# Attention's low product with 64 weight columns, and transposes set between matrix products

## The chip, the cores and the metric

The kernel runs on one core of a Trainium2 chip. The metric is the device time of one execution in microseconds (us), as the median of several runs. A profiled execution of the same program gives the span from its first to its last instruction and the times of every instruction; TensorE's instructions stand there as two rows of work, the matrix products (PE) and their weight loads (PEld).

## The reference

Attention whose mask comes from hash buckets, and behind it two feed-forward blocks with full matrices:

```python
q_bits = (np.einsum('bhsd,dk->bhsk', q, proj) > 0)      # 6 bits, likewise for k
mask = q_bucket[:, :, :, None] == k_bucket[:, :, None, :]
scores = scale * np.matmul(q, k.transpose(0, 1, 3, 2))   # 2 x 8 heads, 768 x 768, head size 64
scores = np.where(mask, scores, -1000000000.0)
attn = np.exp(scores - np.max(scores, axis=-1, keepdims=True))
attn = attn / (np.sum(attn, axis=-1, keepdims=True) + 1e-09)
x = np.matmul(attn, v)                                   # -> 1536 tokens x 512
h = np.maximum(x @ w_in, 0.0);  x = h * h @ w_out        # first block, width 2048
h = x @ w_in2;  y = (h / (1 + np.exp(-h))) @ w_out2      # second block
```

## The kernel before

TensorE multiplies operands that were rounded to a shorter format (fp32r). To keep precision the kernel splits a number into a high part and a low part (the rest) and adds the products of the parts.

The 16 heads are worked on as 8 pairs. A pair is 4 units (2 heads, 2 halves of 384 queries), so there are 32 units, and a unit holds three blocks of 128 queries. Attention is a loop over steps d, from -5 to 97, written out by hand; a step issues work of several units at different stages. One ordinary step holds:

- on TensorE: `transp` (L772) of two key blocks g and g+1, each three 128x128 transposes of the exponentials P into one PSUM tile t; then `av` (L793) of two key blocks that were transposed two steps earlier; then `score_mm` (L734), four products for one query block into a PSUM tile s. The mask's bits are extra rows of the second two of these products.
- on VectorE (DVE): `row_max` (L748) of the score tile of the step before, the low parts of two transposed blocks (`t_lo`, L788), and the two small operations of `row_live` (L752, L753).
- on ScalarE (ACT): the high parts of two transposed blocks (`t_hi`, L782), the exponential of one score tile (`score_exp`, L761), whose last instruction reads the accumulated row sums, and after the last key block of a unit a copy of its output (`ob`, L812).

`av` multiplies P's high part th (L801) and its low part tl (L802) by the same weights: v's high half beside v's low half, 64 + 64 = 128 columns. Rows 0 to 63 of the output tile o collect P times v's high half, rows 64 to 127 P times v's low half; two DMAs and a sum add them later.

Once in a pair, in its step `long[d]`, `bits_mm` (L527) computes the hash bits of the next pair: for each half z six products with 48 weight columns, z = 0 into a tile bs and z = 1 into a tile bt (`ops`, L530). VectorE turns them into mask values (`bits_cmp`, L540), and small DMAs put these into the operands of the next pair's scores (`place_bits`, L661). In six of these seven steps TensorE then runs `rb_mm` (L827): six 128x128 transposes that lay the reciprocal row sums of an older pair along the tokens, into a tile rb, which ScalarE copies out (`x_norm`, L842).

The tiles s, bs and rb share one pool of two PSUM buffers (`ps_s`, L466). They take turns: bs takes the buffer of the score tile before last, rb that of the last score tile, and can be written only after `score_exp` has read that tile. Each engine works through its own list in program order. TensorE's list is read ahead of its array, and a wait there holds what stands behind it.

After attention the feed-forward blocks run, in an order that a planner (`Plan`, L53) makes; the change does not touch them.

Of the kernel before, what the change touches and what calls it, by code (L numbers as in the profile page):

```python
# [444 lines left out]
def lsh_attention_moe_moe(ctx, tc, kd, qk, qf, fq, v, pc, wi1, wo1, wi2, wo2, out):  # L445
# [81 lines left out]
    def bits_mm(p):  # L527
# [4 lines left out]
        for z in range(2):  # L532
            for j, (w, x) in enumerate(ops):
                mm(s[z][0:48, 0:QW], w, x[:, z * QW : (z + 1) * QW], start=j == 0, stop=j == 5)  # L534
# [237 lines left out]
    def transp(g, t=None):  # L772
        u, kt = divmod(g, KT)
        if t is None:
            t = ps_t.tile([128, 512], F32, tag="t", name=f"t{g}")
        for j in range(3):
            nc.tensor.transpose(t[:, j * 128 : (j + 1) * 128], P[u, j][:, kt * 128 : (kt + 1) * 128], ident)  # L777
        PT[g] = (t,)
# [14 lines left out]
    def av(g):  # L793
        u, kt = divmod(g, KT)
        p, h, z = u // 4, (u // 2) % 2, u % 2
        if kt == 0:
            otile[u] = ps_o.tile([128, 512], F32, tag="o", name=f"o{u}")
        o = otile[u]
        vv = pair[p]["vv"][:, h * KT + kt].rearrange("p a d -> p (a d)")
        th, tl = PT.pop(g)  # L800
        mm(o[:, 0:QW], vv, th, start=kt == 0, stop=False)  # L801
        mm(o[:, 0:QW], vv, tl, start=False, stop=kt == KT - 1)  # L802
        if kt == KT - 1:
            if p not in xs:
                xs[p] = [a1.tile([128, S], F32, tag=n, bufs=b, name=f"{n}{p}") for n, b in (("ta", 2), ("tb", 1))]
            if u == NU - 1:
                ta, zs = xs[p][0], slice(z * QW, (z + 1) * QW)
                nc.scalar.copy(out=ta[64:128, zs], in_=o[0:64, 0:QW])
                nc.vector.tensor_tensor(out=ta[64:128, zs], in0=o[64:128, 0:QW], in1=ta[64:128, zs], op=ALU.add)
                return  # L810
            ob = a2.tile([128, QW], F32, tag="ob", name=f"ob{u}")
            nc.scalar.copy(out=ob, in_=o[:, 0:QW])  # L812
            for i in range(2):
                nc.sync.dma_start(out=xs[p][i][64 * h : 64 * h + 64, z * QW : (z + 1) * QW], in_=ob[64 * i : 64 * i + 64])
# [11 lines left out]

    def rb_mm(p):  # L827
        s = ps_s.tile([128, 2, 512], F32, tag="s", name=f"rb{p}")
# [3 lines left out]
        return s  # L832
# [97 lines left out]
    with tc.manual_schedule():  # L930
# [66 lines left out]
        for d in range(-5, G // 2 + 3):  # L997
# [10 lines left out]
            for fn, a in mid.pop(d, []):  # L1008
                fn(*a)
            if 0 <= g < G and d in (92, 94):  # L1010
# [114 lines left out]
```

## Time and profile before

| what | value |
|---|---|
| median of 3 runs | 740.75 us (740.70 to 743.93) |
| span of the profiled execution | 739.4 us |
| PE, PEld busy | 732.1 us (99%), 627.3 us (85%) |
| DVE, ACT, POOL busy | 610.0 us (83%), 461.6 us (62%), 249.6 us (34%) |
| `av`, high part L801 | 192 products, 72.5 us busy |
| `av`, low part L802 | 192 products, 64.5 us busy |
| transposes of P, L777 | 576, 79.1 us busy |
| transposes of `rb_mm`, L831 | 42, 5.7 us busy |
| products of `bits_mm`, L534 | 84 |
| attention's last TensorE work, feed-forward's first | about 235.6 us into the span |
| TensorE clock granted | full in all of 40 slices |

Busy times of products overlap, since each is shown from its start to the modelled end of a pipeline; the distance from one start to the next is what one costs. In a row of several like instructions ("x6") the time runs from the first start to the last end.

### The profile page before, as it was taken

What the parts mean: (1) busy time and instruction counts of PE and PEld (TensorE: products, weight loads), DVE (VectorE), ACT (ScalarE), POOL (GpSimd) and SP (SyncE); (2) the same over time, 40 slices, a digit from 0 to 9 for tenths busy, and PEclk for the clock granted to TensorE, in tenths of its full rate; (3) what the DMA queues carried; (4) which work ended last, traced back from release to release, by engine and by line L of the source; (5) the groups of instructions that cost most, each with busy time, mean ns of one, the idle gap of its engine ahead of it and who ended that gap; (6) DMA issues with size and microseconds to landing.
All of it is one profiled execution on the core that took longest, in us unless ns stands there. A gap on an engine that the chain in (4) does not pass through costs nothing.

```text
span 739.4 us, 10895 instructions
## 1 busy us (share of the span) xinstructions
PE 732.1 (99%) x3734; PEld 627.3 (85%) x3735; DVE 610.0 (83%) x1152; ACT 461.6 (62%) x866; POOL 249.6 (34%) x219
## 2 busy tenths in 40 slices
PE   8999999999999999999999999999999999999998
PEld 4799999999998888888888888888888888888887
DVE  6899999999999998887878896788888777776442
ACT  7888998998896882773566278366335525623510
POOL 7547477877674104103103103500330320230000
PEclk9999999999999999999999999999999999999999
DMA  6987787686462113311320220002133024010012
GB/s 180 210 175 151 182 186 176 154 186 148 115 157 60 57 60 111 114 59 57 114 86 24 91 86 28 29 28 87 58 99 129 30 78 150 1 58 1 1 71 100
DMA packets 27687, 71.87 MB, mean 97 GB/s; under 512 B 4208, under 2 KB 9120, under 8 KB 27632
## 3 DMA queue, kind: packets, MB, share of 16 engines
q1 hardware_dynamic: 24872, 64.52, 31.4%
q0 software_dynamic: 2160, 5.90, 3.9%
q10 hardware_dynamic: 600, 0.75, 0.4%
q8 instruction: 30, 0.49, 0.3%
q14 instruction: 25, 0.20, 0.1%
HBM read 49.80 MB, written 3.15 MB: 72 GB/s over the span
## 4 chain that ended last, share of the span: by engine, by line
PE 95%; DVE 2%; DMA 2%; ACT 1%; issue 0%; SPq 0%; DVEq 0%; ACTq 0%
PE bank L341 35%; PE bank L260 21%; PE bank L231 12%; PE s L741 8%; PE t L777 8%; PE o L802 4%; PE o L801 4%; PE bt L534 1%; DMA fr<-in_dram 1%; PE bs L534 1%; DMA kk<-bt 1%; PE rb L831 1%; DVE tl L788 1%; DVE mt L748 1%; ACT P L761 0%
## 5 line engine op out<-in xcount | busy, mean ns | idle before, releaser
L160 POOL TENSOR_TENSOR wp<-wt,wp 128x512 fp32r<-128x512 f32 x56 | 78.2, 1407 | 329.5 <-ACT wp L158 307.5
L260 PE MATMUL bank<-xb,wp 128*128 128x512 f32 x480 | 110.1, 389 | 0.0
L788 DVE TENSOR_TENSOR tl<-t,th 128x384 fp32r<-128x384 f32 x192 | 104.8, 548 | 2.4 <-ACT th L782 2.2
L260 PEld LDWEIGHTS bank<-xb,wp 128*128 128x128 f32 x480 | 90.1, 188 | 18.7
L761 ACT ACTIVATE P<-s,mt 128x768 f32<-128x768 f32 x96 | 95.6, 996 | 10.6 <-DVE mt L753 7.1
L748 DVE TENSOR_REDUCE mt<-s 128x1 f32<-128x768 f32 x96 | 91.4, 952 | 5.5 <-PE s L741 4.9
L741 PE MATMUL s<-kk,qq 76*128 76x384 f32 (+1 forms) x384 | 84.5, 341 | 1.6 <-DMA kk<-bt 0.8
L782 ACT CAST th<-t 128x384 fp32r<-128x384 f32 x192 | 82.2, 483 | 4.0 <-PE t L777 3.4
L158 ACT CAST wp<-wt 128x512 fp32r<-128x512 f32 x56 | 34.2, 619 | 78.2 <-DVE wt L215 44.5
L231 PE MATMUL bank<-x0h,wp 128*128 128x512 f32 x256 | 80.2, 389 | 0.0
L777 PE MATMUL t<-ident,P 128*128 128x128 f32 x576 | 79.1, 272 | 1.0 <-DVE tl L788 0.9
L777 PEld LDWEIGHTS t<-ident,P 128*128 128x128 f32 x576 | 67.8, 140 | 5.7 <-DVE tl L788 1.1
L801 PE MATMUL o<-th,vv 128*128 128x384 f32 x192 | 72.5, 377 | 0.0
L741 PEld LDWEIGHTS s<-kk,qq 76*128 76x128 f32 (+1 forms) x384 | 67.8, 188 | 4.3 <-ACT P L761 2.1
L265 DVE TENSOR_TENSOR ts<-bank,ts 128x512 f32<-128x512 f32 x80 | 54.4, 690 | 19.8 <-PE bank L260 17.2
L802 PE MATMUL o<-tl,vv 128*128 128x384 f32 x192 | 64.5, 336 | 0.2 <-DVE tl L788 0.2
L245 ACT ACTIVATE ts<-bank 128x512 f32<-128x512 f32 x48 | 28.6, 596 | 49.4 <-PE bank L260 28.9
L231 PEld LDWEIGHTS bank<-x0h,wp 128*128 128x128 f32 x256 | 48.1, 188 | 9.9
L160 DVE TENSOR_TENSOR gql<-ts,gqh 128x512 fp32r<-128x512 f32 x64 | 43.8, 703 | 8.9 <-ACT gqh L158 8.9
L173 ACT ACTIVATE wt<-raw 128x512 f32<-128x512 f32 x58 | 38.1, 671 | 20.2 <-POOL wp L160 17.6
L341 PE MATMUL bank<-wol,gqh 128*128 128x512 f32 (+1 forms) x132 | 50.5, 383 | 0.0
L341 PE MATMUL bank<-woh,gql 128*128 128x512 f32 (+1 forms) x132 | 50.5, 383 | 0.0
(185 smaller groups left out, 1631.7 us busy)
## 6 DMA issues: line engine op xcount, KB each, us to landing
raw<-in_dram SPq DMA_DIRECT2D x64, 512.0 KB
kk<-in_dram POOLq DMA_DIRECT2D x15, 384.0 KB, 6.1
qq<-hq SPq DMA_DIRECT2D x28, 192.0 KB
vr<-in_dram SPq DMA_DIRECT2D x8, 384.0 KB
ta<-ob SPq DMA_DIRECT2D x31, 96.0 KB
tb<-ob SPq DMA_DIRECT2D x31, 96.0 KB
out_dram<-ts SPq DMA_DIRECT2D x11, 256.0 KB
rq<-in_dram SPq DMA_DIRECT2D x7, 384.0 KB
```

The lines of the kernel that those rows point to most:

```text
L160: add(("DVE", "POOL")[pool], l, lambda: eng.tensor_tensor(out=lo(), in0=src(), in1=hi().bitcast(F32), op=ALU.subtract), (*rk, *hk), lk, po ...
L231: mm(bank[b], w[:, x, op, sl], t["x0"][y][:, kt], start=kt == 0 and j == 0, stop=kt == 3 and j == 2)
L260: mm(bank[b], w[:, p, op, k * 128 : k * 128 + 128], x[:, q, xop, k], start=first and k == 0 and j == 0, stop=k == 1 and j == 2, skip_group ...
L341: mm(bank[b][:, 0:wd], x, y, start=i == 0 and n == 0, stop=i == FB - 1 and n == 2)
L741: mm(s[:, n, 0:QW], t["qq"][h][0:kk, ab, c0 : c0 + 128], t["kk"][h][0:kk, ab, n * QW : (n + 1) * QW], start=ab == 0, stop=ab == 1)
L748: nc.vector.tensor_reduce(out=m[:, 0:1], in_=s[:, :, 0:QW], op=ALU.max, axis=AX.XY, negate=True)
L761: nc.scalar.activation(out=e.rearrange("p (a b) -> p a b", a=2), in_=s[:, :, 0:QW], func=AF.Exp, scale=m[:, 1:2], bias=m[:, 2:3], accum_ou ...
L777: nc.tensor.transpose(t[:, j * 128 : (j + 1) * 128], P[u, j][:, kt * 128 : (kt + 1) * 128], ident)
L782: nc.scalar.copy(out=th, in_=PT[g][0][:, 0:QW])
L788: nc.vector.tensor_tensor(out=tl, in0=t[:, 0:QW], in1=th.bitcast(F32), op=ALU.subtract)
L801: mm(o[:, 0:QW], vv, th, start=kt == 0, stop=False)
L802: mm(o[:, 0:QW], vv, tl, start=False, stop=kt == KT - 1)
```

## The change

The two products of `av` are taken apart. `av_hi` is the old product of P's high part with 128 weight columns. `av_lo` multiplies P's low part by v's high half alone, 64 weight columns into the upper 64 rows of o; the product of the two low parts is no longer computed. `av_out` is the rest of `av`.

In 92 steps the order on TensorE becomes another: the three transposes of block g and the first of block g+1 as before, then `av_hi` of the first block, a transpose, `av_lo` of the first, a transpose, `av_lo` of the second, and `av_hi` of the second behind all of them. In steps 92 and 94, and where no transposes are left, the order is high, low, low, high.

`rb_mm` becomes a generator. Where it shares a step with `bits_mm`, one of its six transposes is issued ahead of each of the six products of the half z = 1; where it does not, all six follow as before.

```diff
--- before.py
+++ after.py
@@ -524,13 +524,15 @@
         nc.sync.dma_start(out=t["qq"][h][0:64, 1, :].bitcast(F32), in_=t["lp"][rows, 0].bitcast(F32))
         nc.sync.dma_start(out=t["kk"][h][64:128, 0, :].bitcast(F32), in_=t["lp"][rows, 1].bitcast(F32))
 
-    def bits_mm(p):
+    def bits_mm(p, between):
         t = pair[p]
         hp, lp = t["hp"], t["lp"]
         ops = [(w[:, 48 * i : 48 * i + 48], x) for i in range(2) for (w, x) in ((pjh, hp[i]), (pjl, hp[i]), (pjh, lp[:, i]))]
         s = ps_s.tile([128, 2, 512], F32, tag="s", name=f"bs{p}")[:, 0], ps_t.tile([128, 512], F32, tag="t", name=f"bt{p}")
         for z in range(2):
             for j, (w, x) in enumerate(ops):
+                if z:
+                    next(between, None)
                 mm(s[z][0:48, 0:QW], w, x[:, z * QW : (z + 1) * QW], start=j == 0, stop=j == 5)
         return s
 
@@ -769,12 +771,14 @@
 
     PT = {}
 
-    def transp(g, t=None):
+    def transp(g, t=None, lows=()):
         u, kt = divmod(g, KT)
         if t is None:
             t = ps_t.tile([128, 512], F32, tag="t", name=f"t{g}")
         for j in range(3):
             nc.tensor.transpose(t[:, j * 128 : (j + 1) * 128], P[u, j][:, kt * 128 : (kt + 1) * 128], ident)
+            if j < len(lows):
+                lows[j]()
         PT[g] = (t,)
 
     def t_hi(g):
@@ -790,28 +794,38 @@
 
     xs = {}
 
-    def av(g):
+    def av_at(g):
         u, kt = divmod(g, KT)
         p, h, z = u // 4, (u // 2) % 2, u % 2
+        return u, kt, p, h, z, pair[p]["vv"][:, h * KT + kt]
+
+    def av_hi(g):
+        u, kt, p, h, z, vv = av_at(g)
         if kt == 0:
             otile[u] = ps_o.tile([128, 512], F32, tag="o", name=f"o{u}")
+        mm(otile[u][:, 0:QW], vv.rearrange("p a d -> p (a d)"), PT[g][0], start=kt == 0, stop=kt == KT - 1)
+
+    def av_lo(g):
+        u, kt, p, h, z, vv = av_at(g)
+        mm(otile[u][0:64, 0:QW], vv[:, 0], PT[g][1], start=False, stop=False)
+
+    def av_out(g):
+        u, kt, p, h, z, _ = av_at(g)
         o = otile[u]
-        vv = pair[p]["vv"][:, h * KT + kt].rearrange("p a d -> p (a d)")
-        th, tl = PT.pop(g)
-        mm(o[:, 0:QW], vv, th, start=kt == 0, stop=False)
-        mm(o[:, 0:QW], vv, tl, start=False, stop=kt == KT - 1)
-        if kt == KT - 1:
-            if p not in xs:
-                xs[p] = [a1.tile([128, S], F32, tag=n, bufs=b, name=f"{n}{p}") for n, b in (("ta", 2), ("tb", 1))]
-            if u == NU - 1:
-                ta, zs = xs[p][0], slice(z * QW, (z + 1) * QW)
-                nc.scalar.copy(out=ta[64:128, zs], in_=o[0:64, 0:QW])
-                nc.vector.tensor_tensor(out=ta[64:128, zs], in0=o[64:128, 0:QW], in1=ta[64:128, zs], op=ALU.add)
-                return
-            ob = a2.tile([128, QW], F32, tag="ob", name=f"ob{u}")
-            nc.scalar.copy(out=ob, in_=o[:, 0:QW])
-            for i in range(2):
-                nc.sync.dma_start(out=xs[p][i][64 * h : 64 * h + 64, z * QW : (z + 1) * QW], in_=ob[64 * i : 64 * i + 64])
+        del PT[g]
+        if kt < KT - 1:
+            return
+        if p not in xs:
+            xs[p] = [a1.tile([128, S], F32, tag=n, bufs=b, name=f"{n}{p}") for n, b in (("ta", 2), ("tb", 1))]
+        if u == NU - 1:
+            ta, zs = xs[p][0], slice(z * QW, (z + 1) * QW)
+            nc.scalar.copy(out=ta[64:128, zs], in_=o[0:64, 0:QW])
+            nc.vector.tensor_tensor(out=ta[64:128, zs], in0=o[64:128, 0:QW], in1=ta[64:128, zs], op=ALU.add)
+            return
+        ob = a2.tile([128, QW], F32, tag="ob", name=f"ob{u}")
+        nc.scalar.copy(out=ob, in_=o[:, 0:QW])
+        for i in range(2):
+            nc.sync.dma_start(out=xs[p][i][64 * h : 64 * h + 64, z * QW : (z + 1) * QW], in_=ob[64 * i : 64 * i + 64])
 
     def norm_sums(p):
         nc.gpsimd.tensor_scalar(out=sums[p], in0=sums[p], scalar1=1e-9, scalar2=None, op0=ALU.add)
@@ -824,12 +838,14 @@
 
     rows = {}
 
+    rb_tile = {}
+
     def rb_mm(p):
-        s = ps_s.tile([128, 2, 512], F32, tag="s", name=f"rb{p}")
+        s = rb_tile[p] = ps_s.tile([128, 2, 512], F32, tag="s", name=f"rb{p}")
         for c in range(6):
             o = s[:, c // 3, c % 3 * 128 : c % 3 * 128 + 128]
             nc.tensor.transpose(o, rows[p][:, c].rearrange("p h d -> p (h d)"), ident)
-        return s
+            yield
 
     def x_sum(p):
         ta, tb = xs[p]
@@ -1007,6 +1023,8 @@
                 row_live(m)
             for fn, a in mid.pop(d, []):
                 fn(*a)
+            ns = [n for n in (g - V_LAG, g + 1 - V_LAG) if 0 <= n < G]
+            gone = []
             if 0 <= g < G and d in (92, 94):
                 t = ps_s.tile([128, 2, 512], F32, tag="s", name=f"t{g}")
                 for i in range(2):
@@ -1018,7 +1036,9 @@
                 transp(g)
                 t_hi(g)
                 t_lo(g)
-                transp(g + 1)
+                if len(ns) == 2:
+                    gone = [(av_hi, ns[0]), (av_lo, ns[0]), (av_lo, ns[1])]
+                transp(g + 1, None, [partial(*x) for x in gone])
                 t_hi(g + 1)
             more = extra.pop(d, [])
             if ready and more and d not in long:
@@ -1027,12 +1047,17 @@
                 score_exp(*ready, m)
                 if d in scale:
                     scale_q(scale.pop(d))
-            for n in (g - V_LAG, g + 1 - V_LAG):
-                if 0 <= n < G:
-                    av(n)
+            for fn, n in [x for n in ns[:1] for x in ((av_hi, n), (av_lo, n))] + [x for n in ns[1:] for x in ((av_lo, n), (av_hi, n))]:
+                if (fn, n) not in gone:
+                    fn(n)
+            for n in ns:
+                av_out(n)
+            between = (None for pe, _, p in more for _ in pe(p))
             if d in long:
-                t = bits_mm(long[d])
-            held = [(dve, pe(p), p) for pe, dve, p in more]
+                t = bits_mm(long[d], between)
+            for _ in between:
+                pass
+            held = [(dve, rb_tile[p], p) for _, dve, p in more]
             if d in long:
                 bits_cmp(t, long[d], 0)
                 t_lo(g + 1)
```

TensorE's list around the step that reads unit 5's exponentials (P5) and works on the output tile o4, before. t is a transpose tile, s a score tile, th and tl the high and low parts:

```order
L777 MATMUL t32_850<-ident_89,P5_0_698 128x128 [waits DVE_49,PE_49]
L777 MATMUL t32_850<-ident_89,P5_1_732 128x128
L777 MATMUL t32_850<-ident_89,P5_2_766 128x128
L777 MATMUL t33_858<-ident_89,P5_0_698 128x128 [waits DVE_49]
L777 MATMUL t33_858<-ident_89,P5_1_732 128x128
L777 MATMUL t33_858<-ident_89,P5_2_766 128x128
L801 MATMUL o4_797<-th28_787,vv1_490 128x384
L802 MATMUL o4_797<-tl28_789,vv1_490 128x384
L801 MATMUL o4_797<-th29_795,vv1_490 128x384
L802 MATMUL o4_797<-tl29_815,vv1_490 128x384
L741 MATMUL s7_0_876<-kk1_1_564,qq1_1_563 128x384 [waits Activation_49]
L741 MATMUL s7_0_876<-kk1_1_564,qq1_1_563 128x384 x3
```

The same step of the changed kernel (its line numbers differ; L806 is `av_hi`, L810 `av_lo`):

```order
L779 MATMUL t32_850<-ident_89,P5_0_698 128x128 [waits DVE_49,PE_49]
L779 MATMUL t32_850<-ident_89,P5_1_732 128x128
L779 MATMUL t32_850<-ident_89,P5_2_766 128x128
L779 MATMUL t33_858<-ident_89,P5_0_698 128x128 [waits DVE_49]
L806 MATMUL o4_793<-th28_787,vv1_490 128x384
L779 MATMUL t33_858<-ident_89,P5_1_732 128x128
L810 MATMUL o4_793<-tl28_789,vv1_490 64x384
L779 MATMUL t33_858<-ident_89,P5_2_766 128x128
L810 MATMUL o4_793<-tl29_815,vv1_490 64x384
L806 MATMUL o4_793<-th29_799,vv1_490 128x384
L743 MATMUL s7_0_876<-kk1_1_564,qq1_1_563 128x384 [waits Activation_49]
L743 MATMUL s7_0_876<-kk1_1_564,qq1_1_563 128x384 x3
```

The second and third transposes of t33 now stand behind three more products; the fourth transpose, with its wait for VectorE, stands where it stood.

TensorE's list in a step with `bits_mm` and `rb_mm` before (rb0 is the tile of the six transposes, rw0 the reciprocal row sums, bs2 and bt2 the tiles of the mask bits):

```order
L534 MATMUL bs2_910<-lp2_568,pjh_93 48x384 [waits Pool_49]
L534 MATMUL bt2_911<-hq2_493,pjh_93 48x384 [waits DVE_49,PE_49]
L534 MATMUL bt2_911<-hq2_493,pjl_94 48x384
L534 MATMUL bt2_911<-lp2_568,pjh_93 48x384
L534 MATMUL bt2_911<-hk2_494,pjh_93 48x384
L534 MATMUL bt2_911<-hk2_494,pjl_94 48x384
L534 MATMUL bt2_911<-lp2_568,pjh_93 48x384
L831 MATMUL rb0_924<-ident_89,rw0_812 128x128 [waits PE_49,Activation_49,Pool_49]
L831 MATMUL rb0_924<-ident_89,rw0_812 128x128 x5
L741 MATMUL s7_1_937<-kk1_1_564,qq1_1_563 128x384 [waits DVE_49]
```

And in the changed kernel (L536 is `bits_mm`, L847 `rb_mm`):

```order
L536 MATMUL bs2_910<-lp2_568,pjh_93 48x384 [waits Pool_49]
L847 MATMUL rb0_918<-ident_89,rw0_812 128x128 [waits PE_49,Activation_49,Pool_49]
L536 MATMUL bt2_911<-hq2_493,pjh_93 48x384 [waits DVE_49]
L847 MATMUL rb0_918<-ident_89,rw0_812 128x128
L536 MATMUL bt2_911<-hq2_493,pjl_94 48x384
L847 MATMUL rb0_918<-ident_89,rw0_812 128x128
L536 MATMUL bt2_911<-lp2_568,pjh_93 48x384
L847 MATMUL rb0_918<-ident_89,rw0_812 128x128
L536 MATMUL bt2_911<-hk2_494,pjh_93 48x384
L847 MATMUL rb0_918<-ident_89,rw0_812 128x128
L536 MATMUL bt2_911<-hk2_494,pjl_94 48x384
L847 MATMUL rb0_918<-ident_89,rw0_812 128x128
```

The first transpose of rb0, with its waits for ScalarE (Activation) and GpSimd (Pool), now stands ahead of the first product of bt2 and no longer behind the last.

## Rows read from the trace of the kernel before

**Rows 1.** The page's first part: busy time, share of the span, instructions.
```profile
PE 732.1 (99%) x3734; PEld 627.3 (85%) x3735; DVE 610.0 (83%) x1152; ACT 461.6 (62%) x866; POOL 249.6 (34%) x219
```

**Rows 2.** Chain of waits, end of attention and later: start, us, what.
```profile
191.06 0.66 PE t L777 x6
...
194.46 1.04 PE bs L534 x6
195.50 1.05 PE bt L534 x6
196.55 0.66 PE rb L831 x6
...
235.64 10.90 PE bank L231 x48
```

**Rows 3.** Timeline of PE, two narrow windows in one step: start, us.
```profile
202.08 0.49 PE L777 MATMUL t<-ident,P 128*128 128x128 f32 x3
...
202.19 0.49 PE L777 MATMUL t<-ident,P 128*128 128x128 f32 x3
```

**Rows 4.** Timeline of the weight loads, a narrow window in the same step.
```profile
202.13 0.14 PEld L777 LDWEIGHTS t<-ident,P 128*128 128x128 f32 x1
```

**Rows 5.** Weight loads by line and shape: count, busy us, mean ns, idle us.
```profile
L777 PEld LDWEIGHTS t<-ident,P 128*128 128x128 f32 x576 | 67.8, 140 | 5.7 <-DVE tl L788 1.1 <-DVE ys L844 0.3
...
L801 PEld LDWEIGHTS o<-th,vv 128*128 128x128 f32 x192 | 36.3, 189 | 0.4 <-ACT ob L812 0.4
...
L534 PEld LDWEIGHTS bs<-lp,pjh 128*48 128x48 f32 x14 | 1.7, 122 | 0.7
```

**Rows 6.** Line L831: min, median, max ns; first and last start.
```profile
L831 PEldq EVENT_SEMAPHORE  x7: 968/1177/1178, 57.4 to 226.6; - x7
```

**Rows 7.** Timeline of ACT, then of PE, in the first step with rb.
```profile
57.42 1.00 ACT L761 ACTIVATE P<-s,mt 128x768 f32<-128x768 f32 x1
58.32 0.19 ACT L761 ACTIVATION_READ_ACCUMULATOR P<-s,mt 128x1 f32 x1
...
57.98 0.33 PE L534 MATMUL bt<-hq,pjh 128*48 128x384 f32 x1
```

**Rows 8.** Timeline of the weight loads, the fourth such step.
```profile
142.09 0.48 PEld L741 LDWEIGHTS s<-kk,qq 128*128 128x128 f32 x3 [0.21 <-DVE bt L540]
```

**Rows 9.** Timeline of DVE, one ordinary step.
```profile
202.06 0.96 DVE L748 TENSOR_REDUCE mt<-s 128x1 f32<-128x768 f32 x1
202.94 0.55 DVE L788 TENSOR_TENSOR tl<-t,th 128x384 fp32r<-128x384 f32 x1
203.40 0.14 DVE L752 TENSOR_SCALAR mt<-mt 128x1 f32<-128x1 f32 x1
...
203.58 0.55 DVE L788 TENSOR_TENSOR tl<-t,th 128x384 fp32r<-128x384 f32 x1
204.12 0.96 DVE L748 TENSOR_REDUCE mt<-s 128x1 f32<-128x768 f32 x1
```

**Rows 10.** Timeline of ACT and of the weight loads, behind a unit's end.
```profile
201.37 0.48 ACT L812 COPY ob<-o 128x384 f32<-128x384 f32 x1
...
202.63 0.20 ACT L761 ACTIVATION_READ_ACCUMULATOR P<-s,mt 128x1 f32 x1
...
203.05 0.19 PEld L741 LDWEIGHTS s<-kk,qq 128*128 128x128 f32 x1
```

**Rows 11.** Timeline of DVE and ACT, the last step with rb.
```profile
196.78 0.66 DVE L540 TENSOR_SCALAR bt<-bt,tmt 48x384 fp32r<-48x384 f32 x1
197.94 0.96 DVE L748 TENSOR_REDUCE mt<-s 128x1 f32<-128x768 f32 x1 [0.50 <-PE s L741]
...
197.47 0.76 ACTq L661 DMA_DIRECT2D kk<-bt  x1
```

**Rows 12.** DMA from 196 to 202 us: busy tenths in 40 slices.
```profile
DMA  7976100000000000000925720000000000000000
```

**Rows 13.** Timeline of the weight loads, the last `av` of attention.
```profile
234.54 0.19 PEld L802 LDWEIGHTS o<-tl,vv 128*128 128x128 f32 x1 [0.17 <-DVE tl L788]
```

## The prediction

> **What bounds the kernel now.** I read the page's busy times first, then the chain of waits, then the timelines of one ordinary step and of one step with `rb_mm`. TensorE is busy for 99% of the span [rows 1]. The chain stays on TensorE from piece to piece through attention and goes over to the feed-forward part at 235.6 us without a break [rows 2]; that part, some 504 us, is not touched. So the change is worth what it takes from or adds to TensorE's list in the first 236 us, as long as no other engine becomes late. VectorE is close to that: in an ordinary step its operations stand 0.88 (row maximum), 0.46 (low part), 0.18 (the two small ones) and 0.54 us (low part, up to the next row maximum) apart, 2.06 us together, which is also TensorE's step [rows 9]. A low part that nothing holds takes 0.46, so VectorE alone could do a step in 1.98 us.
>
> **What the low product saves.** It streams 384 columns of P as before. That a product with fewer weight columns costs the same is seen on `bits_mm`: six products with 48 weight columns take 1.04 to 1.05 us, 0.174 each [rows 2], against some 0.17 for one of `av`. Only its weight load gets shorter. Loads of 48 and 128 columns last 122 and 189 ns [rows 5], which is 0.84 ns a column and a fixed part of 82; one of 64 columns would last some 136, by 53 ns less. This is worth something only where a load is not covered by the work ahead of it. Ahead of the first `av` product stands a transpose, and six of those cost 0.66 us, 0.11 each [rows 2], with the 128-column load that follows included. A load's moving part is 189 - 82 = 107 ns, so it just fits behind a transpose. Old cost of that place: nothing that shows; new cost: nothing. **Saving 0.**
>
> **What setting transposes between products saves.** If a transpose took its 0.11 us because its own load holds it, a product of 0.17 us ahead of it would hide that load. The rows say no. Its load lasts 140 ns, 58 above the fixed part, so about half of 0.11 [rows 5]. And in the step at 202 us the fourth transpose's load is late: the third transpose starts at 202.08, that load at 202.13, the fourth transpose at 202.19 [rows 3, 4]. It starts 0.06 us after its load and still 0.11 after the transpose before it. So a transpose occupies the array for 0.11 us itself, whoever stands next. Lower bound of what two transposes per step could save, if it were otherwise: a 512-column product costs 10.90/48 = 0.227 [rows 2], so 128 columns cost 0.227 - 0.174 = 0.053, and each transpose ahead of a narrow load could save 0.11 - 0.053 = 0.057, 10.5 us in 2 x 92 places. Upper bound of a loss: more changes between transposes and products, four in a step; the six transposes' 0.66 us hold some 0.01 us beyond six times 0.109, so at most 4 x 0.007 x 92 = 2.6 us. I take **+0.3 us**, near no change, because the load row speaks plainly.
>
> The Trainium skill (TensorE: Matmul & The Clock Gate, LDWEIGHTS) has a load take its columns over 1.2 GHz, 53 ns for 64 and 107 for 128. By it a transpose's own 128 columns would be its limit, which is rival 1. The trace agrees for the plain loads (0.84 ns a column) and not for a transpose's, whose row has half of that.
>
> **What moves beside them.** The second and third transposes of block g+1 come behind three products, and the last of them 3 x 0.174 = 0.52 us later less the two products that now stand behind: 0.35 us later. Its high part on ScalarE starts some 0.04 us later than now in an ordinary step and 0.3 later in one with an output copy; that copy, at 201.37, is then 0.08 late, and so is the exponential behind it. Its last reader, the row sums' read, ends at 202.83, and the load of the score that needs the buffer stands at 203.05 [rows 10]. That cover of 0.2 us holds; without it 31 units x 0.08 = 2.5 us. I cost it at 0. The fourth transpose, which waits for VectorE with 0.05 us to spare, has kept its place.
>
> **What the new place of `rb_mm` adds.** Its first transpose waits for ScalarE: rb takes the buffer of the last score tile, and the exponential of that tile must have been read. Now that transpose comes after `bits_mm`, and the wait is hidden. It is in the trace all the same: TensorE's reader of its list sits in it for 1.18 us, from 57.4 to about 58.55 [rows 6], and that is some 0.04 after the read of the row sums ends at 58.32 + 0.19 = 58.51 [rows 7]. The products of `bits_mm` were already handed over by then. In the changed list this transpose stands ahead of bt's first product, which starts at 57.98 [rows 7]. So TensorE arrives there at 57.98, the wait ends at 58.55, the load and the start behind it take some 0.09 (0.06 from load to start, rows 4 and 3): start at 58.64, **0.66 us of idle TensorE**. All behind it, five transposes, six products, the score, is in one list and comes as much later. The exponential cannot come earlier: it follows the row maximum and the row's small operations, on a score tile that TensorE made before. Six steps have this form; the wait's median is 1177 ns and the largest 1178, the least (968) belongs to the later step that has no `bits_mm` [rows 6], so all six are alike: 6 x 0.66 = **+4.0 us**. In one of them TensorE loses a part today: the load at 142.09 waits 0.21 us for `bits_cmp` of the first half [rows 8], and the idle time now put ahead covers that: **-0.25 us**, with what its product lost behind it.
>
> Who waits for it: bt is complete 1.1 us later (0.66 and four to five transposes), so VectorE's second comparison moves from 196.78 to about 197.87 and ends its turn at 198.45, ahead of the row maximum (197.94 + 0.66 = 198.60), which already waits for TensorE [rows 11]. The DMA of the bits moves from 197.47 to about 198.55 [rows 11]; the transfer is over at 199.6 today [rows 12] and would be at 200.7, with the score that needs it at 201.5 + 0.66. Covered. That issue holds ScalarE for 0.76 us, to 199.3, where the next high part could start at 199.0: 0.3 us that the exponential's wait behind it takes up. A cover gone would cost up to 0.3 x 6 = 1.8 us.
>
> **The end of attention.** The last low product waits for VectorE, its load starts at 234.54 [rows 13]. The last high product now stands behind it and no longer ahead: 0.17 us, less 0.05 for the shorter load: **+0.1 us**.
>
> **The sum**: 4.0 - 0.25 + 0.3 + 0.1 = +4.1 us. The profiled execution goes from 739.4 to 743.5 us of span; the median of the runs lies 1.35 us above that span (740.75), which I add again: **744.8 us**.
>
> **Rivals.**
> 1. Transposes between products do save. For it: no row here shows a narrow load right behind a transpose; against it: the late load that delays nothing [rows 3, 4]. TensorE could win 10.5 us, but VectorE's 1.98 us a step ends it: 0.08 x 92 = 7 us at most, some 6 with the other work of that engine. With 4.1 lost elsewhere less 6 x 0.3 for rb's own transposes, the time is 740.75 - 6 + 4.1 - 1.8 = about 737 (to 739.5 where it saves half). It is faster from the point where each moved transpose saves over 0.025 us. Chance 0.11.
> 2. The idle time at rb is not passed on, because another engine had been late by as much in these steps. For it: VectorE's 1.98 of 2.06 us leave it little room [rows 9]. Against it: the row maximum behind such a step waits 0.50 us for TensorE, so VectorE is not the late one there [rows 11]; TensorE has no idle time after these steps that could take the loss back, and the 0.25 us lost at 142 us today is not caught up. Half of it passed on: 742.7. Chance 0.10.
> 3. rb's wait is not met there (another buffer, an earlier exponential): only the small terms stay, 741.1. The list's wait for ScalarE stands in the new place word for word, so chance 0.04.
> 4. A change of weight width stops the array: each of four changes in a step would cost a product's way through, 0.33 - 0.17 = 0.16 us, 0.16 x 4 x 92 = 59 us slower, 800. Against it: `av` (128) to `bits_mm` (48) and on to `rb_mm` (128) shows no gap in the chain [rows 2]. Chance 0.01. The Trainium skill (TensorEngine Tiling (Array Packing), Key Properties) says that changing the tiling mode drains the array; by the sum with that rule it would be this rival, and the trace does not agree for 48 columns.
>
> **How the numbers follow.** The forecast's mechanism has 0.74, with a range of its own of 743.6 to 746.2 (0 to 1.6 us for the changes of kind, a little for ScalarE's late work). A measurement of this kernel tells some 0.5%, 3.7 us, from no change; that line is at 744.45, close to my forecast. Of the 0.74, 0.46 lie above it and 0.28 below. With rival 4: slower 0.47. Same: 0.28 and rivals 2 and 3, 0.14, and 0.05 of rival 1: 0.47. Faster, under 737.05: the other 0.06. The range that leaves out the far part of rival 1 and the upper end beyond the covers: 739.8 to 746.3.
>
> **What would show it.** In the profile after: the first transpose of each of six rb tiles starts behind an idle time of about 0.65 us that ended with ScalarE's exponential, and VectorE's row maximum waits there as much longer; transposes between products keep about 0.11 us, low products 0.17; ordinary steps keep 2.05 us, and the feed-forward part starts at about 239.7 us. Wrong would be: steps under 2.0 us (rival 1), no idle time at rb (rival 3), or idle time at rb with the later steps catching up (rival 2).

## The result and the profile after

The changed kernel takes 745.29 us (median of 7 runs, 744.65 to 748.45); the kernel before, run beside it, 740.59. The ratio is 1.0065, with a 95% interval of 1.0044 to 1.0086: slower by 4.7 us. 744.8 had been forecast. The profiled execution has a span of 743.5 us for 739.4.

The page's first part of the kernel after, against [rows 1]: engine, busy us, share of the span, instructions.

```profile
PE 733.6 (99%) x3734; PEld 623.4 (84%) x3735; DVE 611.3 (82%) x1152; ACT 464.9 (63%) x866; POOL 249.7 (34%) x219
```

TensorE is still at 99%, with 1.5 us more of busy time in a span that is 4.1 longer. The total can't say where that comes from; the steps can. First, an ordinary step. The timeline of PE after: start, us, engine, line, operation, tiles, how many (the length of a row is the time until its last one has gone through the array, so rows overlap; the distance of the starts is what the array gives to each).

```profile
203.55 0.60 PE L779 MATMUL t<-ident,P 128*128 128x128 f32 x4
203.91 0.42 PE L806 MATMUL o<-th,vv 128*128 128x384 f32 x1
204.17 0.27 PE L779 MATMUL t<-ident,P 128*128 128x128 f32 x1
204.20 0.42 PE L810 MATMUL o<-tl,vv 128*64 128x384 f32 x1
204.45 0.27 PE L779 MATMUL t<-ident,P 128*128 128x128 f32 x1
204.48 0.41 PE L810 MATMUL o<-tl,vv 128*64 128x384 f32 x1
204.74 0.34 PE L806 MATMUL o<-th,vv 128*128 128x384 f32 x1
204.91 0.86 PE L743 MATMUL s<-kk,qq 128*128 128x384 f32 x4
```

The next step begins at 205.61, so this one has 2.06 us, as before. From 204.17 to 204.45 a transpose and a narrow product take 0.28 us together, which is the 0.11 of the one and the 0.17 of the other in the old order. Neither the 64 weight columns nor the neighbours have changed what the array gives to an instruction. The start of a row is not its share: the product at 204.20 starts 0.03 behind the transpose, but keeps what comes next waiting for 0.25.

Now the first step with `rb_mm`, against [rows 7]. PE after:

```profile
57.32 0.33 PE L536 MATMUL bs<-lp,pjh 128*48 128x384 f32 x1
58.10 0.30 PE L847 MATMUL rb<-ident,rw 128*128 128x128 f32 x1 [0.45 <-issue]
...
59.85 0.87 PE L743 MATMUL s<-kk,qq 128*128 128x384 f32 x4
```

And ACT in the same step:

```profile
56.92 0.99 ACT L763 ACTIVATE P<-s,mt 128x768 f32<-128x768 f32 x1
57.81 0.19 ACT L763 ACTIVATION_READ_ACCUMULATOR P<-s,mt 128x1 f32 x1
```

The last product of `bs` starts at 57.32, and the next instruction could follow 0.17 later. It is rb's first transpose, and it starts at 58.10, 0.10 behind the end of ScalarE's read of the row sums (57.81 + 0.19). From 57.32 to the score at 59.85 are 2.53 us; the seven products (0.174 each) and six transposes (0.11) in between need 1.88. So 0.65 us are lost. In all six of these steps rb's first transpose starts 0.10 us behind the end of that read, and in five of them 0.64 to 0.66 us are lost. The idle time in the bracket, 0.45, is smaller than the loss: it counts from the end of the product's way through the array, and in a list without a hole that way is covered by the next instruction.

The bracket also says "issue" and not ScalarE. The wait is not on the transpose but on an instruction of its own ahead of it, which the list's reader has to get past; the answer for line L847 after shows it (min, median and max ns), against [rows 6]:

```profile
L847 PEldq EVENT_SEMAPHORE  x7: 51/1852/1855, 56.2 to 231.5; - x7
```

The reader sits there for 1.85 us in place of 1.18. Before, it had handed over the products of `bt` by then, and the array lived on those; now it has only the rest of `bs`.

The sixth of these steps is longer than the others. The chain of waits after, there:

```profile
198.36 0.62 POOL wp L719
...
199.06 0.30 PE rb L847
```

and ACT:

```profile
197.84 1.03 ACT L763 ACTIVATE P<-s,mt 128x768 f32<-128x768 f32 x1
198.72 0.23 ACT L763 ACTIVATION_READ_ACCUMULATOR P<-s,mt 128x1 f32 x1
```

The profile puts the end of the wait down to a cast on GpSimd, which ends at 198.98. ScalarE's read ends just ahead of it, and rb starts as far behind that read as in the first step (0.10). So the read explains it here as well, and the name in the chain is that of the operation that happened to end last. The loss is 0.73 us here. Against TensorE's list the exponential starts 0.05 us later than in the first step (0.35 us ahead of the last product of `bs` and not 0.40), and from its start to the end of the read it takes 1.11 us for 1.08.

DVE in that step, against [rows 11]:

```profile
200.99 0.67 DVE L542 TENSOR_SCALAR bt<-bt,tmt 48x384 fp32r<-48x384 f32 x1 [1.20 <-PE bt L536]
201.70 0.96 DVE L750 TENSOR_REDUCE mt<-s 128x1 f32<-128x768 f32 x1
```

VectorE's second comparison now waits 1.20 us for `bt`; the row maximum, which waited 0.50 before, follows it without a wait that shows.

Placing the last score of each of the 96 steps on both traces gives the sum. Up to step 12 the kernel after is 0.56 us *ahead*: the profile of before has a wait of 0.8 us for a DMA at 36.6 us that this one does not have. The six steps with rb then add 0.70, 0.69, 0.67, 0.43, 0.68 and 0.81, together 3.98 us; the other steps 0.45; the end of attention 0.21. That makes 4.08 us up to the first product of the feed-forward part, and 4.64 without the difference at the start, which is near what the medians show (4.70).

### The profile page after: what moved, and what is told of

Same layout as the page of the kernel before. It is cut to its first block, busy times and chain, and to the rows that moved or that the text cites. A ratio compares the mean times of both kernels' runs of the same rounds, so it can differ in the third digit from the quotient of the medians.

```text
span 743.5 us, 10866 instructions
## 1 busy us (share of the span) xinstructions
PE 733.6 (99%) x3734; PEld 623.4 (84%) x3735; DVE 611.3 (82%) x1152; ACT 464.9 (63%) x866; POOL 249.7 (34%) x219
## 4 chain that ended last, share of the span: by engine, by line
PE 90%; DVE 7%; ACT 1%; issue 1%; DMA 0%; POOL 0%; ACTq 0%
PE bank L341 35%; PE bank L260 20%; PE bank L231 12%; PE s L743 7%; PE t L779 6%; DVE mt L750 3%; PE o L806 3%; PE o L810 3%; DVE tl L792 3%; PE bt L536 1%; PE bs L536 1%; PE rb L847 1%; PE warm L734 1%; DVE mt L755 0%; ACT P L763 0%
## 5 line engine op out<-in xcount | busy, mean ns | idle before, releaser
L779 PE MATMUL t<-ident,P 128*128 128x128 f32 x576 | 108.9, 272 | 1.0 <-DVE tl L792 0.9
L786 ACT CAST th<-t 128x384 fp32r<-128x384 f32 x192 | 87.6, 484 | 8.4 <-PE t L779 3.7
L779 PEld LDWEIGHTS t<-ident,P 128*128 128x128 f32 x576 | 76.5, 140 | 5.3 <-DVE tl L792 1.1
L806 PE MATMUL o<-th,vv 128*128 128x384 f32 x192 | 72.5, 379 | 0.2 <-ACT ob L826 0.2
L810 PE MATMUL o<-tl,vv 128*64 128x384 f32 x192 | 67.1, 417 | 0.1
```

The costliest lines, as they stand in the source:

```text
L786: nc.scalar.copy(out=th, in_=PT[g][0][:, 0:QW])
L806: mm(otile[u][:, 0:QW], vv.rearrange("p a d -> p (a d)"), PT[g][0], start=kt == 0, stop=kt == KT - 1)
L810: mm(otile[u][0:64, 0:QW], vv[:, 0], PT[g][1], start=False, stop=False)
```

## The experiments

All were timed in five rounds against the kernel before, whose median was 740.54, 740.46 and 740.31 us in the three groups of runs.

**1. rb's transposes behind bits_mm again**, all else as in the changed kernel (`rb_behind`):

```diff
-                if z:
-                    next(between, None)
```

> The changed kernel with its six rb transposes behind bits_mm again, all else kept. Wait theory (the transposes stand in front of bt's products and wait for the exponential, 0.66 us in six steps): the idle time at rb is gone, 741.3 to 741.7 us, 3.6 to 4.0 below the changed kernel. Rival (changes between transposes and products in the 92 ordinary steps cost the time): 744.5 us or more.

Measured: 741.43 us, ratio 1.0012 (1.0003 to 1.0021). One edit of two lines takes back 3.9 of the 4.7 us. The line of rb there waits 1.28 us in the reader's list, and the array does not notice:

```profile
L845 PEldq EVENT_SEMAPHORE  x7: 51/1277/1280, 56.0 to 227.0; - x7
```

**2. The other half alone: the kernel before, with only rb's transposes amid bits_mm** (`rb_amid_only`; the low product is whole and the transposes of P stand together):

> The kernel before with only the new place of the rb transposes, av as before. Wait theory: 740.6 + 6 x 0.66 - 0.25 = 744.3 us (744.0 to 744.8), with 0.65 us of idle time ahead of the first transpose of six rb tiles. Rival (the ordinary steps' new order or the narrow product cost the time): 740.6 to 741.2 us.

Measured: 744.43 us, ratio 1.0058 (1.0042 to 1.0074). PE in one of its six steps:

```profile
200.48 0.34 PE L536 MATMUL bs<-lp,pjh 128*48 128x384 f32 x1
201.28 0.30 PE L835 MATMUL rb<-ident,rw 128*128 128x128 f32 x1 [0.47 <-issue]
```

The same hole, 0.80 us between two starts that would be 0.17 apart, without any of the other edits. The two experiments agree from both sides: 3.9 us with all else changed, 3.9 with nothing else changed.

**3. The same interleaving, but later** (`rb_late`): the first three transposes ahead of the fifth product of `bt`, the rest ahead of the sixth.

```diff
-                if z:
-                    next(between, None)
+                if z and j >= 4:
+                    for _ in range(3):
+                        next(between, None)
```

> The changed kernel, but the six rb transposes stand three ahead of the fifth and three ahead of the sixth product of the half z = 1: still amid products, but TensorE comes to them some 0.70 us later than in the changed kernel, when the exponential has just been read (0.66). Wait theory: no or under 0.1 us of idle time at rb, 741.4 us (741.0 to 742.0). Rival (a transpose amid narrow products is dear by itself): about 745 us, as the changed kernel.

Measured: 741.51 us, ratio 1.0015 (1.0007 to 1.0023). So transposes amid these products are not dear as such; what costs is that the first of them stands before the products that used to hide its wait.

**4. The low product with all 128 weight columns**, in the order of experiment 1 (`low_128`; it computes P's low half times v's low half again):

```diff
-        mm(otile[u][0:64, 0:QW], vv[:, 0], PT[g][1], start=False, stop=False)
+        mm(otile[u][:, 0:QW], vv.rearrange("p a d -> p (a d)"), PT[g][1], start=False, stop=False)
```

> rb transposes behind bits_mm as in rb_behind, the new order of the ordinary steps kept, but av_lo with all 128 weight columns (so the product of the two low parts is computed again). My theory (a load of 128 columns fits behind a transpose of 0.11 us): as rb_behind, 741.5 us, at most 1.3 more (0.007 in 2 x 92 places). Rival (64 columns are what hides the load behind a transpose): 53 ns in 184 places, 9.8 us over rb_behind, 751 us.

Measured: 741.21 us, ratio 1.0012 (1.0004 to 1.0020), against 741.43 with 64 columns. Twice the weight behind a transpose costs nothing. Its weight loads by line and shape (count, busy us, mean ns, idle us before them):

```profile
L808 PEld LDWEIGHTS o<-tl,vv 128*128 128x128 f32 x192 | 36.2, 189 | 3.1 <-DVE tl L790 0.6
```

The same row of the kernel after:

```profile
L810 PEld LDWEIGHTS o<-tl,vv 128*64 128x64 f32 x192 | 26.0, 136 | 5.8 <-DVE tl L792 0.7
```

Each load became 53 ns shorter, some 10 us in all, and no product comes sooner for it. The idle time ahead of these loads grew by 2.7 us; most of the rest had lain beside neighbouring loads, whose rows overlap: from 40 to 220 us the loader is busy for 170.3 us in `low_128` and for 168.5 in `rb_behind`.

**5. Where do the other 0.9 us come from?** Two kernels were to say. `no_amid` is experiment 1 with P's transposes together again (`gone = []`), so that only the products' order and their width are new. `low_64_only` is the kernel before with nothing but the narrow low product (in the last block of a unit it stands ahead of the high one).

> The changed kernel with rb's transposes behind bits_mm, and block g+1's transposes one behind the other again, ahead of all four products; the order of the products (high, low, low, high) and the narrow low products stay. That kernel without this second edit took 741.4 us, 0.9 over the kernel before. If the transposes between products cost that, this one takes 740.5; if the order of the products does (the last high product behind the low one), it stays at 741.4. The theory that changes between transposes and products cost a little (0.007 us in each place) says 740.7.

> The kernel before in its own order; only the low product has 64 weight columns (P's low half times v's low half is left out). Theory (a narrow weight is worth nothing, its load is covered): 740.5 us, the same as before within 0.1%. Rival (a narrow weight pays only where no transpose stands ahead of its load, so the changed order hid its gain): some 192 x 0.02 us or more less, 737 or lower.

Measured: `no_amid` 741.83 us, ratio 1.0023 (1.0011 to 1.0036); `low_64_only` 741.97, ratio 1.0017 (1.0009 to 1.0026). Both expectations of a single culprit failed: the transposes' place is not it, and the narrow product alone, expected at 740.5, is no better than the rest. With experiments 1, 3 and 4 (the last with 128 columns, 0.7 over the kernel before) every kernel with these edits of `av` and without the early rb transposes stands 0.7 to 1.5 us above the kernel before. All of them share one thing, the high product as the last of a unit; it stands in every third step, while all three steps of a unit are longer. Their traces show some 0.01 us a step, medians of 2.060 to 2.076 for 2.053, and no wait for it: the distances between products are some nanoseconds longer, as in the scores of `no_amid`, whose four products take 540 ns from the first start to the last where the kernel before has 521 (medians). Why is open.

**6. Can narrow products be worth something at all?** Two products with 64 weight columns each use half of the array. In `bf_halves` the two low products of a step follow each other, the even block's into partitions 0 to 63 of `o`, the odd block's into 64 to 127. Both operands are in bfloat16: P's low half is written so, and v has a copy in it. No run has this form in fp32r. `bf_same` is the same with both in partitions 0 to 63. rb is behind bits_mm in both. The line of the product:

```diff
-        mm(otile[u][0:64, 0:QW], vv[:, 0], PT[g][1], start=False, stop=False)
+        r = 64 * (kt % 2)          # bf_same: r = 0
+        mm(otile[u][r : r + 64, 0:QW], pair[p]["vb"][:, h * KT + kt], PT[g][1], start=False, stop=False)
```

> The changed kernel with rb's six transposes behind bits_mm again, and the two low products of a step one behind the other, in bfloat16 (P's low half and a copy of v's high half rounded to it): the product of the even block goes to partitions 0 to 63 of the output tile, that of the odd block to partitions 64 to 127, which the sum of the two halves at the end makes the same. So both use 64 columns of the array, each its own. Theory (a product costs TensorE its 384 streamed columns whatever its weight columns, one product at a time): no gain, 741.4 us, a little more if the casts on GpSimd are in the way. Rival (two products in different columns of the array run side by side, and the narrow weight then is worth a whole product): TensorE's step falls by 0.17 us to 1.88, VectorE's operations hold it at 1.98, some 0.07 x 92 = 6.4 us less: 735. Second rival (changing between the whole array and its halves costs a wait each time): over 745.

> The same as the kernel with the halves, but both low products go to partitions 0 to 63, so that they use the same columns of the array: all that is left is the other number format. Both theories: 741.4 us, as with rb's transposes behind bits_mm; a time below 740 would say that bfloat16 itself is what helps, and then the kernel with the halves shows nothing of the array's columns.

Measured: `bf_halves` 749.37 us, ratio 1.0116 (1.0103 to 1.0129); `bf_same` 763.41, ratio 1.0304 (1.0291 to 1.0318). Neither is the 741.4 that was expected of the theory; the second rival, a wait at each change between the whole array and its halves, had said over 745. The low products, by line and shape, in `bf_halves`:

```profile
L811 PE MATMUL o<-tl,vb 128*64 128x384 bf16 x190 | 33.6, 350 | 0.0
```

and in `bf_same`:

```profile
L811 PE MATMUL o<-tl,vb 128*64 128x384 bf16 x176 | 45.1, 338 | 0.0
```

(190 and 176 of 192 rows are in this window.) With different columns of the array, 95 pairs are busy for 33.6 us, 0.35 a pair, which is hardly more than one product lasts (350 ns): the two run side by side. With the same columns a pair takes 45.1/88 = 0.51, one behind the other. So there the narrow weight is worth a product. PE of `bf_halves` in a step shows why it is slower all the same:

```profile
206.48 0.60 PE L779 MATMUL t<-ident,P 128*128 128x128 f32 x4
...
207.10 0.27 PE L779 MATMUL t<-ident,P 128*128 128x128 f32 x1
207.30 0.35 PE L811 MATMUL o<-tl,vb 128*64 128x384 bf16 x2
207.59 0.33 PE L779 MATMUL t<-ident,P 128*128 128x128 f32 x1
207.67 0.43 PE L806 MATMUL o<-th,vv 128*128 128x384 f32 x1
207.94 0.86 PE L743 MATMUL s<-kk,qq 128*128 128x384 f32 x4
208.63 0.60 PE L779 MATMUL t<-ident,P 128*128 128x128 f32 x4
```

and the weight loads of the same place:

```profile
207.30 0.11 PEld L811 LDWEIGHTS <-vb 128*64 128x64 bf16 x2 [0.21 <-issue]
207.58 0.14 PEld L779 LDWEIGHTS t<-ident,P 128*128 128x128 f32 x1 [0.17 <-issue]
```

In the kernel after, a low product starts 0.03 us behind the transpose ahead of it, and its load runs still earlier. Here the first bfloat16 load starts at 207.30, when the transpose of 207.10 is three quarters through, and the load of the next float32 transpose at 207.58, when the two products are nearly through (207.30 + 0.35). The loader stands idle twice, and the array loses time by it: the transpose ahead of the pair keeps it for 0.20 us (0.11 elsewhere), the pair for 0.29 (0.17 for one product), and the transpose and the high product behind it for 0.35 (0.28). That is 0.28 us more, where two products side by side save one, 0.17; the step has 2.15 us (206.48 to 208.63) for 2.06. No semaphore is waited for: "issue" is all the profile has for it, and the 64-column product in fp32r does not show it. `bf_same` pays the same and saves nothing, 22 us.

Is it the other format that costs this, or the half array? The first steps of the kernel before have the two apart. There a product in bfloat16 with all 128 weight columns (L732, on a dummy tile) stands between a score and the transposes:

```profile
19.73 0.33 PE L741 MATMUL s<-kk,qq 76*128 76x384 f32 x1
19.90 0.39 PE L732 MATMUL warm<-zero 128*128 128x512 bf16 x1
20.13 0.60 PE L777 MATMUL t<-ident,P 128*128 128x128 f32 x4
```

The distances are 0.17 and 0.23 us, what 384 and 512 columns take elsewhere (0.174 and 0.227): going into bfloat16 and back cost the array nothing. And the first hash bits (L641) go from 128 rows of the array to 64, in fp32r throughout (64*24 stands for 64 rows and 24 weight columns):

```profile
12.99 0.34 PE L641 MATMUL bs<-kk,pjd 128*24 128x384 f32 x1
...
13.26 0.35 PE L641 MATMUL bs<-kk,pjd 64*24 64x384 f32 x1
```

with the weight load of the second:

```profile
13.26 0.10 PEld L641 LDWEIGHTS bs<-kk,pjd 64*24 64x24 f32 x1 [0.28 <-issue]
```

Here the distance is 0.27 us for 0.17, and the load starts late as in `bf_halves`. So the rows put the price on changing between the whole array and a half of it, and not on the format. Why 64 columns in fp32r do not pay it is open: no run has 64 columns in both formats with all else alike.

**7. One visit to the half array for three steps.** `bf_six` puts the six low products of a unit together, ahead of the unit's last high product. `bf_even` also moves the high products: three in each of the first two steps, none beside the six low ones. Both have 11 buffers for the low parts in place of 6. A part of the first edit:

```diff
-            for fn, n in [x for n in ns[:1] for x in ((av_hi, n), (av_lo, n))] + [x for n in ns[1:] for x in ((av_lo, n), (av_hi, n))]:
-                if (fn, n) not in gone:
-                    fn(n)
+            for n in ns:
+                if n % KT == KT - 1:
+                    for i in range(KT):
+                        av_lo(n - KT + 1 + i)
+                av_hi(n)
```

> Low products in bfloat16 in the two halves of the output tile as in the kernel with the halves, but the six of a unit stand together, ahead of the unit's last high product, so that TensorE goes into bfloat16 and back once in three steps and not in each; rb behind bits_mm, the transposes together. From the two kernels with the halves and with the same half: side by side saves (763.41 - 749.37)/96 = 0.146 us a step, and what is left of the 749.37 against 741.43 is a change of format of 0.083 + 0.146 = 0.23 us. Theory (the change of format is paid once per visit): a unit of three steps takes 0.23 - 3 x 0.146 = -0.21 us, 31 units -6.5: 735, if VectorE's 1.98 us a step leave it that. Rival (steps of uneven length: two of 1.70 us and one of 2.46, and VectorE, which needs 1.98 in each and is at most 0.2 us behind or ahead, can't even them out): 6.2 us a unit for the 6.16 of before: 742 to 744. Second rival (the change of format costs by the product, not by the visit): 749.

> As the kernel with six low products together, and the high products moved so that the three steps of a unit are nearly alike for TensorE: three high products in the first, three in the second (the last two a step sooner), in the third the six low ones alone. By rows of the kernels before: 6 transposes 0.66, 4 scores 0.69, a product 0.174: steps of 1.87, 1.87 and 1.35 + 3 x 0.20 + 0.23 = 2.18, 5.92 us for 6.16. Theory (visit, and evenness): VectorE's 1.98 us a step decides, 5.94 to 6.1 a unit: 735 to 739, and at least 3 us under the kernel with the six where that one is uneven. Rival (the change of format costs by the product): 749. Rival (a high part that is needed a step sooner makes TensorE wait for ScalarE): idle time ahead of the high products that ended with ScalarE, over 741.

Measured: `bf_six` 750.67 us, ratio 1.0139 (1.0125 to 1.0153); `bf_even` 741.50, ratio 1.0011 (1.0000 to 1.0023). PE of `bf_six` in the long step of a unit:

```profile
213.38 1.06 PE L779 MATMUL t<-ident,P 128*128 128x128 f32 x6
...
214.55 0.68 PE L809 MATMUL o<-tl,vb 128*64 128x384 bf16 x6
215.16 0.44 PE L804 MATMUL o<-th,vv 128*128 128x384 f32 x1
...
216.13 0.82 PE L779 MATMUL t<-ident,P 128*128 128x128 f32 x6
```

Six low products in 0.61 us (214.55 to 215.16), 0.10 each in place of 0.17. But the step has 2.75 us, and its transposes take 1.06 for 0.82, since the fourth waits for a low part of VectorE. DVE's row maxima in the same unit:

```profile
211.78 0.95 DVE L750 TENSOR_REDUCE mt<-s 128x1 f32<-128x768 f32 x1
213.75 0.95 DVE L750 TENSOR_REDUCE mt<-s 128x1 f32<-128x768 f32 x1
216.33 0.96 DVE L750 TENSOR_REDUCE mt<-s 128x1 f32<-128x768 f32 x1 [0.52 <-PE s L743]
```

They stand 1.97 us apart in a short step, which is VectorE's own time, and 2.58 in the long one, where it waits 0.52 for TensorE. What the short steps leave TensorE in hand is lost: 2 x 1.97 + 2.58 = 6.52 us a unit, where three steps of before take 6.16. This is the rival of uneven steps, dearer than it had been priced (6.2). PE of `bf_even`:

```profile
205.20 0.92 PE L779 MATMUL t<-ident,P 128*128 128x128 f32 x6
206.05 0.68 PE L809 MATMUL o<-tl,vb 128*64 128x384 bf16 x6
206.66 0.98 PE L743 MATMUL s<-kk,qq 128*128 128x384 f32 x4
207.47 0.82 PE L779 MATMUL t<-ident,P 128*128 128x128 f32 x6
```

Its step with the low products takes 2.27 us, not the 2.18 of the expectation: 0.85 up to the first of them, 0.61, and 0.81 for the scores, which take 0.70 elsewhere. In the two others VectorE holds TensorE, at 1.97 to 1.99 us a step. DVE of `bf_even`:

```profile
207.67 0.96 DVE L750 TENSOR_REDUCE mt<-s 128x1 f32<-128x768 f32 x1 [0.18 <-PE s L743]
...
209.66 0.95 DVE L750 TENSOR_REDUCE mt<-s 128x1 f32<-128x768 f32 x1
```

From 207.67 it goes on to 209.66, 211.63 and 213.86: 6.19 us a unit. TensorE has less to do than before, and the end comes at the same time, because VectorE loses in one step what it can't win in the next. That the change is paid once a visit is borne out (for `bf_even` the rival of a price by the product had said 749), and that VectorE ends the gain too; the 735 to 739 us were not reached. The expectations call the change one of format, which the rows of experiment 6 do not bear out. No version beat the kernel before.

## Why the prediction was right

- **Saving of the low product, 0.** Right. The load took 136 ns, as worked out from 122 and 189 [rows 5], and experiment 4 shows that no product comes later where the load is 53 ns longer. "Takes the same for fewer weight columns", read from `bits_mm` [rows 2], holds for 64.
- **Transposes between products save 0.** Right in the mechanism: 0.11 and 0.17 us in each pair, and `no_amid` without them is no faster. For the +0.3 us taken for changes of kind the kernel after has 0.45 over all steps without rb. The reason given for it is not borne out: `low_64_only`, which has no more such changes than the kernel before, is 1.5 us above it.
- **What moves beside them, 0.** Right as far as rows go: the weight loads of scores wait for ScalarE four times in all, 2.5 us for 2.1 before, and ordinary steps keep 2.06 us.
- **The wait at rb, 6 x 0.66 us.** Right, and this decided. The first one lost 0.65, by its 13 instructions, and the steps grew by 0.67 to 0.70 where nothing else was in play; in `rb_behind` the same steps, without the hole, grew by up to 0.03. The term taken back at 142 us is there: that step grew by 0.43 and not by 0.68. In its weight loads, against [rows 8], the score has no wait left and rb has one:

```profile
142.49 0.14 PEld L847 LDWEIGHTS rb<-ident,rw 128*128 128x128 f32 x1 [0.82 <-issue]
...
144.09 0.72 PEld L743 LDWEIGHTS s<-kk,qq 128*128 128x128 f32 x4
```

 Not all six were alike: the sixth grew by 0.81. Its hole is 0.08 longer, by the later and longer exponential, and its first high product comes 0.07 later, just behind an output copy on ScalarE (195.76 + 0.48, product at 196.30). And one sign that had been named did not come: not the row maximum waits longer on VectorE, but the second comparison, by 1.20 us, and the row maximum behind it no more.
- **The end of attention, +0.1 us.** 0.21. The weight loads after, against [rows 13]:

```profile
238.04 0.13 PEld L810 LDWEIGHTS o<-tl,vv 128*64 128x64 f32 x1 [0.35 <-DVE tl L792]
238.50 0.13 PEld L810 LDWEIGHTS o<-tl,vv 128*64 128x64 f32 x1 [0.33 <-DVE tl L792]
```

 The high product that used to fill such a wait stands behind it, as the step says; it happens at two products, not at one.
- **The sum.** The span of 743.5 us was met to a tenth, and a part of that is luck: the start of the profiled execution was 0.56 us shorter, and the terms 0.54 larger (3.98 + 0.45 + 0.21 for 4.1).
- **The rivals.** Rival 1 falls with the ordinary step, which keeps 2.06 us, and with `no_amid` (741.83 us without transposes between products, 741.43 with them). Rival 2, the hole not passed on, falls with the six steps, each of which stays longer, and with experiments 1 and 2. Rival 3 falls with the rows of L847. Rival 4 falls for fp32r: pairs of 128 and 64 columns take their plain 0.28 us. For this the Trainium skill (TensorEngine Tiling (Array Packing), Key Properties) was cited with the drain of the array at a change of tiling mode; no row here shows one at 48 or 64 columns in fp32r, while the rows of experiment 6 agree with it for 64 columns in bfloat16 and for 64 rows in fp32r. Its sentence that different tiles can run in parallel the trace confirms, with 0.35 us a pair in `bf_halves`.

## What to carry to other kernels

A wait in an in-order list is free as long as the work *already handed over* ahead of it keeps the engine busy: before moving an instruction ahead of others, look at whether its own semaphore wait was being hidden by exactly those others, even where the profile shows no idle time at it (a wait of 1.18 us here cost nothing, and the same wait a few instructions earlier cost 0.66). Fewer weight columns saved TensorE nothing here, where the streamed columns stayed and the load was covered. Where two engines need nearly the same time for a step, relieving one wins at most the difference, and uneven steps lose even that.

## What had not been expected of the hardware

- Two 64-column bfloat16 products into different halves of the partitions run side by side (0.35 us a pair for 0.51), and going to them from the whole array and back holds the weight loads, 0.21 and 0.17 us in the step shown. A product in bfloat16 on the whole array, between float32 and fp32r ones, has no such price (0.17 and 0.23 us), and 64 rows in fp32r have it (0.27 us for 0.17). `bf_same` is 22 us over experiment 1, nearly the same order in fp32r, in 96 steps.
- A chain of waits can move to another engine without the time changing: in the ordinary steps it runs over VectorE in the kernel after (from 205.82 to 207.88 us over the row maximum, a low part, the two small operations and a low part again) and over TensorE before, while the step has 2.05 to 2.06 us in both. Where two engines are nearly equal, the chain names one of them.
- Small edits that leave TensorE's work alike made every one of these kernels 0.1 to 0.2% slower. No run here explains it.
